# Adding exponential tiles on VectorE before the softmax sums, in chosen units of a fused attention + leaky-ReLU MLP kernel

## The chip, the cores and the metric

The kernel runs on one core of one Trainium2 chip. The metric is the device time of one execution in microseconds (us), the median of several runs. Within the core five engines work side by side, each from its own in-order queue of instructions: PE (TensorE, matrix products), DVE (VectorE), ACT (ScalarE), POOL (GpSimd) and SP (which issues DMA here). They meet only through semaphores: an instruction waits until what it needs has been written, or until what it overwrites has been read. Tile pools give each tile a buffer, and a pool with fewer buffers than tiles makes the next user wait for the last one.

## The reference

Eight batches of 12 heads, 448 positions, head width 64; then an MLP from 768 to 2048 and back on the 3584 rows that the attention gives.

```python
def rmsnorm(x, g):
    rms = np.sqrt(np.mean(x * x, axis=-1, keepdims=True) + 1e-06)
    return x / rms * g
q_n, k_n = (rmsnorm(q, g_q), rmsnorm(k, g_k))
scores = 1.0 / np.sqrt(64) * np.matmul(q_n, k_n.transpose(0, 1, 3, 2))
scores = scores - np.max(scores, axis=-1, keepdims=True)
attn = np.exp(scores)
attn = attn / (np.sum(attn, axis=-1, keepdims=True) + 1e-09)
attn_out = np.matmul(attn, v)                      # 8 x 12 x 448 x 64
x = attn_out.transpose(0, 2, 1, 3).reshape(3584, 768)
h = x @ w_in                                       # 768 x 2048
g = np.maximum(0.01 * h, h)
out = g @ w_out                                    # 2048 x 768
```

## The kernel before

The work is cut into 24 units `u` of four heads each (three units make a batch). A unit has seven key tiles; the exponentials of key tile `t` stand in `et[:, t]`, 128 partitions (keys) by 2 x 448 fp16. Units are pipelined: while unit `u` forms scores and exponentials in four steps `d` = 0 to 3 (key tile 0; 1 and 2; 3 and 4; 5 and 6), PE also sums and multiplies the exponentials of unit `u-1`, and in the gaps it runs items of the MLP of an earlier batch from a queue (`fill`). The program order on each engine is fixed by the order of these calls.

The parts that matter here: the softmax sums over keys are matrix products with ones. `zcol` serves units 4 to 22, `zsum_slot` the last (and the first few).

```python
def zcol(u):                       # sums of unit u: 7 tiles x 4 matmuls
    s = st[u]
    s["zc"] = aux([P, 512], FP32, "zc")
    for t in range(NS):            # NS = 7
        for y in range(2):
            for a in range(2):
                c = 32 * (2 * y + a)
                nc.tensor.matmul(s["zc"][c:c + 32, 0:HS], onesr, s["et"][:, t, a, HS * y:HS * y + HS],
                                 start=(t == 0), stop=(t == NS - 1))       # 224 columns each

def shift_max(u):                  # the row shift of unit u, from its first score tile
    ...
    nc.vector.tensor_reduce(s["spare"][:, 511:512], sT[:, :, 0:S], axis=AXL.XY, op=ALU.max)
    s["dg"] = small.tile([P, P], FP16, tag="dg", name="dg")
    nc.vector.tensor_tensor(s["dg"], ident16, s["spare"][:, 511:512].broadcast_to([P, P]), op=ALU.mult)

def shift_mm(u):                   # spreads it over the partitions
    ...
    for x in range(2):
        nc.tensor.matmul(pb[:, x], onesp, s["dg"][:, 64 * x:64 * x + 64], start=True, stop=True)
    nc.vector.tensor_reduce(s["spare"][:, 510:511], pb, axis=AXL.XY, op=ALU.max)
    ...
```

The norms and the scaling of the attention's output on GpSimd:

```python
def prep_rinv(u, tis=BOTH):        # 1/rms on ACT
    nc.scalar.activation(buf(u, "uu")[:, x], buf(u, "ssq")[:, x], AF.Ln, bias=eps_t, scale=1.0 / D)
    nc.scalar.activation(buf(u, "rinv")[:, x], buf(u, "uu")[:, x], AF.Exp, bias=0.0, scale=-0.5)

def prep_norm(u, ...):             # n = x * rinv on DVE, two inputs in SBUF
    nc.vector.tensor_tensor(buf(u, "n16")..., src[...], buf(u, "rinv")...broadcast_to(...), op=ALU.mult)

def xmul_pool(u, eng=nc.gpsimd):   # xt = x32 * rz, two inputs in SBUF
    ...
    eng.tensor_tensor(xts[b][:, g], s["x32"], s["rz"], op=ALU.mult)
```

The second half of the MLP as seven products; `later` puts an evacuation off to the next item, `flush` issues what was put off. The third product adds to the bank `ma` that the copy put off by the first one has to have read:

```python
def i0():
    flush()
    g["o"] = (out_tile(), out_tile())
    mm(bank("ma"), gblock(tt[0], 0), wblock(0, 0), True)
    later(lambda: nc.vector.tensor_copy(g["o"][1][:, L], g["ma"][:, 0:HC]))
def i1():
    flush()
    mm(bank("mb"), sa[:, 1], tw[:, 1], True)
    later(lambda: add(g["o"][1][:, L], g["o"][1][:, L], "mb"))
    ...
def i2():
    flush()
    mm(g["ma"], gblock(tt[0], 1), wblock(1, 0), False)      # accumulates into ma
    ...
```

The loop, cut to what is needed:

```python
for u in range(3, NU):             # NU = 24
    for d in range(4):
        qk(u, STEPS[d])            # scores, PE
        if d == 0:
            shift_max(u)           # DVE
            ...
            pv_slot(u - 1)         # attention times v, PE, 28 matmuls
            zcol(u - 1)            # PE
            shift_mm(u)            # PE, waits for dg
            pv_out(u - 1)          # x32, ACT, waits for the shift
        ex(u)                      # exponentials, ACT
        ...
        jobs = []                  # d == 1: prep_ssq(u+2);  d == 2: prep_rinv(u+2), prep_norm(u+2), its transposes
        ...
        fill(u, d, jobs)           # MLP items from the queue, one job after each
zsum_slot(NU - 1)
pv(NU - 1)
...
```

Of the kernel before, what the change touches and what calls it, by code (L numbers as in the profile page):

```python
# [8 lines left out]
FP32 = mybir.dt.float32  # L9
FP16 = mybir.dt.float16  # L10
AF = mybir.ActivationFunctionType
ALU = mybir.AluOpType
# [6 lines left out]
def kernel(  # L19
# [11 lines left out]
    nc = tc.nc  # L31

    B, H, S, D = q.shape
    QH = 4
    NS = 7
    P = 128
    NQ = H // QH
    NU = B * NQ
# [6 lines left out]
    cst = ctx.enter_context(tc.tile_pool(name="cst", bufs=1))  # L45
# [4 lines left out]
    zpool = ctx.enter_context(tc.tile_pool(name="zpool", bufs=1))  # L50
# [6 lines left out]
    def aux(shape, dtype, name):  # L57
        if held:
            return held[0].pop(0)
        return psum.tile(shape, dtype, tag="aux", bufs=4, name=name)  # L60
# [6 lines left out]
    def drop(bank):  # L67
        if held:
            held[0].append(bank)
# [3 lines left out]
    ones16 = cst.tile([P, D], FP16)  # L73
    nc.vector.memset(ones16, 1.0)
    onesr = cst.tile([P, 32], FP16)
# [6 lines left out]
    nc.vector.memset(eps_t, 1.0e-6)  # L82
    one32 = cst.tile([1, 1], FP32)
    nc.vector.memset(one32, 1.0)
    grow = cst.tile([1, 2, D], FP32)
    gdup = cst.tile([1, 2, D], FP32)
    gcol = cst.tile([P, 1], FP32)
    gate_t = cst.tile([P, 1], FP16)
    vts = [cst.tile([P, 2, NS, D], FP16, name=f"vt{i}") for i in range(NV)]
# [21 lines left out]
    st = {}  # L111
# [51 lines left out]
    def prep_norm(u, c=ALL, tis=BOTH):  # L163
        n = c[1] - c[0]
        for ti in tis:
            src = raw[u][ti]
            nc.vector.tensor_tensor(  # L167
                buf(u, "n16")[:, ti, c[0]:c[1]].rearrange("p s a d -> p a s d"), src[:, :, c[0]:c[1]],
                buf(u, "rinv")[:, ti, :, c[0]:c[1], None].broadcast_to([P, 2, n, D]), op=ALU.mult)
# [19 lines left out]
    def slot():  # L189
        return psum.tile([P, 2, 512], FP32, tag="sT", bufs=2, name="sT")  # L190
# [7 lines left out]
    def qk(u, steps):  # L198
        st[u]["sT"] = []
        for t in steps:  # L200
            sT = slot()
            score(u, t, (sT[:, 0], sT[:, 1]))
            st[u]["sT"].append((t, sT))
# [17 lines left out]
    def shift_max(u):  # L221
        s = st[u]
        sT = s["sT"][0][1]
        if isinstance(sT, list):
            pm2 = small.tile([P, 2], FP32, tag="pm2", name="pm2")
            for a in range(2):
                nc.vector.tensor_reduce(pm2[:, a:a + 1], sT[a][:, 0:S], axis=AXL.X, op=ALU.max)
            s["spare"] = sT[0]
            nc.vector.tensor_reduce(s["spare"][:, 511:512], pm2, axis=AXL.X, op=ALU.max)
        else:  # L230
            s["spare"] = sT[:, 0]
# [3 lines that stand above are left out]
# [25 lines left out]
    def zsum(u, t0=0, t1=NS):  # L260
        s = st[u]
        for t in range(t0, t1):
            for r in range(2):
                for a in range(2):
                    nc.tensor.matmul(s["zt"][r][64 * a:64 * a + 64, 0:S], ones16[64 * r:64 * r + 64],
                                     s["et"][64 * r:64 * r + 64, t, a], start=(t == 0), stop=(t == NS - 1))

    def zsum_slot(u):
        s = st[u]
        s["zslot"] = slot()  # L270
        s["zt"] = [s["zslot"][:, r] for r in range(2)]
        zsum(u)

    HS = S // 2

    def zcol(u):
        s = st[u]
        s["zc"] = aux([P, 512], FP32, "zc")
        for t in range(NS):
            for y in range(2):  # L280
                for a in range(2):
                    c = 32 * (2 * y + a)
                    nc.tensor.matmul(s["zc"][c:c + 32, 0:HS], onesr, s["et"][:, t, a, HS * y:HS * y + HS],  # L283
                                     start=(t == 0), stop=(t == NS - 1))

    def pv_slot(u):
        s = st[u]
        s["pslot"] = slot()
        s["pv"] = [s["pslot"][:, r] for r in range(2)]
        pv(u)  # L290

    def pv_out(u):
        s = st[u]
        s["x32"] = zpool.tile([P, 2, S], FP32, tag="x32", name="x32")
        nc.scalar.copy(s["x32"], s["pslot"][:, :, 0:S])  # L295

    def zcol_ln(u):
        s = st[u]
        s["zs"] = zpool.tile([P, HS], FP32, tag="zs", name="zs")
        nc.scalar.activation(s["zs"], s["zc"][:, 0:HS], AF.Ln)  # L300
        drop(s["zc"])

    def zcol_inv(u):
# [3 lines left out]
        for r in range(2):  # L307
            for y in range(2):
                src = s["zs"][64 * y + r:64 * y + 64:2, None, :]
                nc.sync.dma_start(s["rz"][:, r, HS * y:HS * y + HS], src.broadcast_to([32, 4, HS]))  # L310

    def xmul_sb(u):
        xmul_pool(u, nc.vector)
# [382 lines left out]
    def narrow(u):  # L696
        return 4 <= u < NU - 1
# [46 lines left out]
    with tc.manual_schedule():  # L744
# [182 lines left out]
        for u in range(3, NU):  # L927
            for d in range(4):
                if d > 0 or u > 3:
                    qk(u, STEPS[d])  # L930
                    if d == 0:
                        shift_max(u)
                        if u == 6:
                            xmul_sb(u - 2)
                        if narrow(u - 1):
                            pv_slot(u - 1)
                            zcol(u - 1)
                            shift_mm(u)
                            pv_out(u - 1)
                        else:  # L940
                            zsum_slot(u - 1)
                            pv(u - 1)
                            shift_mm(u)
                            zinv(u - 1)
                    ex(u)
                    if d == 0 and narrow(u - 1):
                        zcol_ln(u - 1)
                jobs = []

                def job(fn, *args):  # L950
                    jobs.append(lambda: fn(*args))

                if d == 0:
                    if u == 3:
                        prep_norm(4)
                        gate(4)
                    elif narrow(u - 1):
                        if u < NU - 1:
                            job(zcol_inv, u - 1)
                    else:  # L960
                        xmul(u - 1)
                    if u + 4 < NU:
                        job(load, u + 4)
                    if u + 3 < NU:
                        load_v(u + 3)
                    if u < 6:
                        prep_sqp(u + 3)
                if d == 1 and narrow(u - 1) and not 5 <= u < 8 and u < NU - 1:
                    xmul_pool(u - 1)
                if u == NU - 1:  # L970
                    if d == 1:
                        job(zcol_inv, u - 1)
                    if d == 2:
                        xmul_pool(u - 1)
                if fed(u, d) and u > 3:
                    push(u // NQ - 1)
                if (u, d) in ((3, 1), (4, 0)):
                    for ti in range(2):
                        prep_tr(u + 1, ti, VV)
                if d == 1 and 5 <= u < NU - 1:  # L980
                    job(prep_g, u + 1)
                if u + 2 < NU:
                    if d == 1:
                        for ti in range(2):
                            job(prep_ssq, u + 2, ALL, (ti,))
                    if d == 2:
                        job(prep_rinv, u + 2)
                        for ti in range(2):
                            job(prep_norm, u + 2, ALL, (ti,))
                        if u > 3:  # L990
                            job(prep_trd, u + 2)
                if d == 1 and 4 <= u < 8:
                    job(weight_sum, u - 4, 0)
                if d == 0 and 5 <= u < 9:
                    job(weight_sum, u - 5, 1)
                if d == 2 and 6 <= u < 8:
                    job(xmul_sb, u - 1)
                if u == NU - 2 and d == 0:
                    for n, tile_ in ((1, (raws, "rq", 3)), (2, (raws, "rk", 3)), (3, None), (4, (prep_p, "sq", 3))):
                        job(win_sum, n, 1, tile_)  # L1000
                    for n in (3, 1, 2, 4):
                        job(x_sum, LATE, n)
                if d == 3 and 6 <= u < NU - 3:
                    for ti in range(2):
                        job(prep_sq, u + 3, ALL, (ti,))
                fill(u, d, jobs)
# [4 lines left out]
        for i, ns in enumerate(((3, 1), (2, 4))):  # L1011
            c, fn = queue[i]
# [33 lines left out]
```

## Time and profile before

| | |
|---|---|
| time, median of 3 runs | 422.28 us (421.82 to 422.55) |
| span of the profiled execution | 420.3 us |
| granted TensorE clock, mean | 0.992 |
| POOL line 320, `xt<-x,rz` | 16 times, 2085 ns each |
| ACT line 214, the exponentials, 128x896 | 166 times, 1010 ns each |
| PE line 283, the sums `zc` | 504 records of 224 columns |

How to read it: the profile is one execution. A group's row names line, engine, operation and tiles, then the busy time, the mean length of one, and the idle time of the engine just before it with the instruction that ended the idle time. The timeline gives start and length in us. Engines run in order, so an idle time on one engine says what it waited for next, not that it had nothing further down its queue. Only what delays the engine that is never idle, or the chain of waits that ends last, changes the time.

### The profile page before, as it was taken

To read this page: it belongs to the slowest core of one execution; us is meant where nothing else is said; L and a number is where in the kernel's file an instruction comes from. 1 tells how busy PE (TensorE), PEld (TensorE's weight loads), DVE (VectorE), ACT (ScalarE), POOL (GpSimd) and SP (SyncE) were. 2 spreads that over 40 slices of the span, in tenths; PEclk is the share of its full clock that TensorE was granted. 3 is DMA by queue.
4 is the path that set the end of the run, shared out by engine and by line. 5 is a ranking of instruction groups with operands and counts; after the bars stand their busy time and mean duration, and the time that the engine had idled before them with its cause. 6 is when DMAs were issued, how large, how long until landed. Compare 5 with 4: busy or idle time off the path is not lost.

```text
span 420.3 us, 9568 instructions
## 1 busy us (share of the span) xinstructions
PE 404.4 (96%) x3959; PEld 222.9 (53%) x3959; DVE 269.2 (64%) x440; ACT 303.6 (72%) x474; POOL 83.0 (20%) x75
## 2 busy tenths in 40 slices
PE   7977999999999999999999999999999999999995
PEld 6544444555445544555445544455445557558853
DVE  5788665787658736466448745467338787527762
ACT  5999878868987689867986779967986657653600
POOL 1958422300020111210121111120101101010000
PEclk9699999999999999999999999999999999999999
DMA  8999999889664795678565796578562460032023
GB/s 257 218 239 237 235 250 147 200 156 215 169 153 68 224 212 120 168 163 180 152 130 107 194 203 150 151 141 170 180 111 44 121 155 11 7 78 75 2 53 100
DMA packets 71951, 62.42 MB, mean 149 GB/s; under 512 B 36324, under 2 KB 67044, under 8 KB 71908
## 3 DMA queue, kind: packets, MB, share of 16 engines
q1 hardware_dynamic: 61312, 49.62, 47.2%
q0 software_dynamic: 10272, 11.80, 18.1%
q8 instruction: 31, 0.51, 0.5%
q10 hardware_dynamic: 324, 0.39, 0.3%
q14 instruction: 12, 0.10, 0.1%
HBM read 45.61 MB, written 11.01 MB: 135 GB/s over the span
## 4 chain that ended last, share of the span: by engine, by line
PE 83%; ACT 8%; DVE 6%; issue 1%; DMA 1%; SPq 0%; DVEq 0%; ACTq 0%
PE hps L362 27%; PE sT L195 8%; PE sT L340 6%; PE ma L444 5%; PE md L444 5%; PE mc L444 5%; ACT et L214 5%; PE bank L444 5%; PE bank L564 4%; PE op L403 3%; PE zc L283 3%; PE mb L444 3%; DVE n L167 2%; PE sT L444 2%; PE bank L403 1%
## 5 line engine op out<-in xcount | busy, mean ns | idle before, releaser
L214 ACT ACTIVATE et<-sT,eb 128x896 f16<-128x896 f32 x166 | 159.4, 1010 | 18.6 <-PE sT L195 16.9
L362 PE MATMUL hps<-xt,win 128*128 128x448 f16 x600 | 120.8, 353 | 0.2 <-DVE xt L349 0.2
L362 PEld LDWEIGHTS <-win 128*128 128x128 f16 x612 | 56.8, 98 | 58.2 <-issue 9.6
L320 POOL TENSOR_TENSOR xt<-x,rz 128x896 f16<-128x896 f32 x16 | 33.4, 2085 | 148.0 <-DMA rz<-zs 139.5
L356 ACT ACTIVATE gt<-hps 128x448 f16<-128x448 f32 x100 | 54.0, 556 | 6.1 <-PE hps L362 5.4
L167 DVE TENSOR_TENSOR n<-rq,rinv 128x896 f16<-128x896 f32 (+2 forms) x25 | 27.2, 1090 | 47.0 <-ACT rinv L161 44.2
L195 PE MATMUL sT<-qkT 64*64 64x448 f16 x664 | 53.2, 369 | 3.0 <-ACT et L214 1.9
L155 DVE TENSOR_REDUCE ssq<-sq 128x14 f32<-128x896 f32 (+2 forms) x49 | 50.3, 1058 | 1.6 <-ACT sq L144 1.6
L444 PEld LDWEIGHTS <-sa 128*128 128x128 f16 x352 | 32.8, 98 | 26.3 <-issue 6.1
L295 ACT COPY x<-sT 128x896 f32<-128x896 f32 x19 | 17.2, 906 | 36.4 <-DVE sT L245 36.4
L124 POOL DMA_DIRECT2D vt<-in_v_dram x24 | 18.2, 757 | 114.9 <-PE sT L340 107.4
L444 PEld LDWEIGHTS <-gt 128*128 128x128 f16 x264 | 25.2, 98 | 18.7 <-issue 2.1
L195 PEld LDWEIGHTS <-qkT 64*64 64x64 f16 x672 | 15.2, 105 | 36.8 <-issue 33.5
L340 PE MATMUL sT<-et,vt 64*64 64x448 f16 x532 | 28.5, 350 | 0.3
L403 PE MATMUL op<-wout,gt 128*128 128x384 f16 x160 | 28.4, 327 | 0.0
L232 DVE TENSOR_REDUCE sT<-sT 128x1 f32<-128x896 f32 x22 | 24.1, 1093 | 4.3 <-PE sT L195 4.3
L340 PEld LDWEIGHTS <-vt 64*64 64x64 f16 x672 | 20.7, 107 | 11.3 <-issue 1.7
L167 DVE TENSOR_TENSOR n<-rk,rinv 128x896 f16<-128x896 f32 (+2 forms) x26 | 26.1, 1009 | 0.0
L403 PEld LDWEIGHTS <-gt 128*128 128x128 f16 x192 | 17.6, 98 | 14.3 <-issue 3.0
L444 PE MATMUL ma<-wout,gt 128*128 128x384 f16 x128 | 23.5, 326 | 0.0
L425 DVE TENSOR_TENSOR sa<-gt 128x512 f16<-128x512 f16 (+1 forms) x15 | 8.2, 544 | 18.5 <-ACT gt L356 13.9
L144 ACT ACTIVATE sq<-rq 128x896 f32<-128x896 f32 (+2 forms) x18 | 16.3, 913 | 1.3 <-DMA rq<-in_q_dram 1.3
(135 smaller groups left out, 516.6 us busy)
## 6 DMA issues: line engine op xcount, KB each, us to landing
rq<-in_q_dram SPq DMA_DIRECT2D x24, 448.0 KB, 3.9
rk<-in_k_dram SPq DMA_DIRECT2D x24, 448.0 KB, 5.6
out_dram<-ost SPq DMA_DIRECT2D x52, 192.0 KB, 3.3
rz<-zs SPq DMA_DIRECT2D x76, 112.0 KB, 2.3
vt<-in_v_dram POOLq DMA_DIRECT2D x24, 224.0 KB, 5.1
win<-in_moe_w_in_dram POOLq DMA_DIRECT2D x8, 384.0 KB, 16.8
wout<-in_moe_w_out_dram POOLq DMA_DIRECT2D x2, 1536.0 KB, 29.7
out_dram<-ost SPq DMA_DIRECT2D x4, 96.0 KB, 2.1
```

The lines of the kernel that those rows point to most:

```text
L124: nc.gpsimd.dma_start(vts[u % NV].rearrange("p a t d -> p a (t d)"), rows(v, u))
L155: nc.vector.tensor_reduce(buf(u, "ssq")[:, ti, :, c[0]:c[1]], buf(u, f"sq{ti}")[:, :, c[0]:c[1]], axis=AXL.X, op=ALU.add)
L167: nc.vector.tensor_tensor(buf(u, "n16")[:, ti, c[0]:c[1]].rearrange("p s a d -> p a s d"), src[:, :, c[0]:c[1]], buf(u, "rinv")[:, ti, :, ...
L195: nc.tensor.matmul(banks[a][64 * r:64 * r + 64, 0:S].rearrange("p (t x) -> p t x", t=NS), kT(u, r, a, t), qT(u, r, a), start=True, stop=True)
L214: nc.scalar.activation(s["et"][:, t], sT[:, :, 0:S], AF.Exp, bias=s["eb"], scale=1.0)
L232: nc.vector.tensor_reduce(s["spare"][:, 511:512], sT[:, :, 0:S], axis=AXL.XY, op=ALU.max)
L320: eng.tensor_tensor(xts[b][:, g], s["x32"], s["rz"], op=ALU.mult)
L340: nc.tensor.matmul(s["pv"][r][64 * a:64 * a + 64, 0:S], vts[u % NV][64 * r:64 * r + 64, a, t], s["et"][64 * r:64 * r + 64, t, a], start=(t ...
L356: nc.scalar.activation(dst, src, AF.Prelu, bias=0.0, scale=1.0, alpha=0.01)
L362: nc.tensor.matmul(hps[:, 0:S], win16[:, kt // 2, kt % 2, ts(ft, P)], xt[:, kt // 2, kt % 2], start=(kt == 0), stop=(kt == KT - 1))
L403: nc.tensor.matmul(op2[:, 0:HC], gt[:, ft, ds(col(t), P)], wout16[:, ft, ds(HC * half, HC)], start=(ft == 0), stop=(ft == FT - 1))
L444: nc.tensor.matmul(bank[:, 0:HC], a[:, f], b[:, f], start=(first and f == 0), stop=(f == HF - 1), skip_group_check=not first)
```

## The change

In twelve units VectorE adds some of the seven exponential tiles into one fp16 tile `ea` first, so that the product with ones has fewer tiles to sum: in nine units five tiles are added (four additions), in three units three tiles (two additions). The product then takes the remaining `et` tiles and `ea` last. It is meant to use time in which VectorE stood idle in step 2 for the norms' reciprocals, and to take matmuls off PE. The sums are those of the same exponentials, with the partial sums rounded to fp16.

```diff
-    grow = cst.tile([1, 2, D], FP32)
-    gdup = cst.tile([1, 2, D], FP32)
+    g_t = zpool.tile([P, 2, S], FP32, tag="x32", name="g_t")          # room for ea
+    grow = g_t[0:1, 0, 0:2 * D].rearrange("p (a d) -> p a d", a=2)
+    gdup = g_t[0:1, 1, 0:2 * D].rearrange("p (a d) -> p a d", a=2)
@@ zsum_slot
-        zsum(u)
+        ets = z_tiles(u)
+        for i, e in enumerate(ets):
+            ... the same matmuls with e in place of et[:, t] ...
@@
+    ADDED = {8: 3, 14: 3, 20: 3, NU - 1: 5}
+    ADDED.update({u: 5 for u in (4, 7, 10, 11, 13, 16, 17, 19)})
+
+    def add_e(u):
+        s = st[u]
+        s["ea"] = zpool.tile([P, 2, S], FP16, tag="ea", name="ea")
+        for t in range(1, ADDED[u]):
+            nc.vector.tensor_tensor(s["ea"], s["et"][:, 0] if t == 1 else s["ea"], s["et"][:, t], op=ALU.add)
+
+    def z_tiles(u):
+        s = st[u]
+        ets = [s["et"][:, t] for t in range(NS)]
+        return ets[ADDED[u]:] + [s["ea"]] if "ea" in s else ets
@@ zcol
-        for t in range(NS):
+        ets = z_tiles(u)
+        for i, e in enumerate(ets):
             for y in range(2):
                 for a in range(2):
                     c = 32 * (2 * y + a)
-                    nc.tensor.matmul(s["zc"][c:c + 32, 0:HS], onesr, s["et"][:, t, a, HS * y:HS * y + HS],
-                                     start=(t == 0), stop=(t == NS - 1))
+                    nc.tensor.matmul(s["zc"][c:c + 32, 0:HS], onesr, e[:, a, HS * y:HS * y + HS],
+                                     start=(i == 0), stop=(i == len(ets) - 1))
@@ the loop, after ex(u)
+                if d == 2 and u in ADDED and u < NU - 1:
+                    add_e(u)
@@ the loop, among the jobs
+                if u == NU - 1 and d == 3:
+                    job(add_e, u)
```

So in units 4 to 20 the additions stand in VectorE's queue at the start of step 2, before the norms of that step; in the last unit they stand in step 3. In the order of instructions of the changed kernel the two additions of units 14 and 20 stand directly after the second `ssq` and before the copy of `ma`, those of unit 8 after that copy and after two of the MLP's block sums, before the addition of `mb`.

More of the change, by code (lines that the diff above doesn't have):

```diff
@@ L271, in zsum_slot @@
         s["zt"] = [s["zslot"][:, r] for r in range(2)]
-        zsum(u)
-    HS = S // 2
+        ets = z_tiles(u)
+        for i, e in enumerate(ets):
+            for r in range(2):
+                for a in range(2):
+                    nc.tensor.matmul(s["zt"][r][64 * a:64 * a + 64, 0:S], ones16[64 * r:64 * r + 64],
+                                     e[64 * r:64 * r + 64, a], start=(i == 0), stop=(i == len(ets) - 1))
+    HS = S // 2
+    ADDED = {8: 3, 14: 3, 20: 3, NU - 1: 5}
[9 more added lines that the diff above has]
+        return ets[ADDED[u]:] + [s["ea"]] if "ea" in s else ets
     def zcol(u):
```

## The prediction

> **What bounds the kernel now.** I read the page's busy shares first, then the chain of waits, then the timeline around one hand-over between units, then the collisions of DVE and POOL.
>
> ```profile
> PE 404.4 (96%) x3959; PEld 222.9 (53%) x3959; DVE 269.2 (64%) x440; ACT 303.6 (72%) x474; POOL 83.0 (20%) x75
> ...
> PE 83%; ACT 8%; DVE 6%; issue 1%; DMA 1%; SPq 0%; DVEq 0%; ACTq 0%
> ```
>
> PE is the bound: 96% busy, 83% of the chain. A matmul taken off PE shortens the time only if PE does not meet another wait instead; and anything that stops PE is added, as it has no slack to catch up with. Each hand-over from unit u to u+1 looks like this one (13 to 14):
>
> ```profile
> 210.50 0.29 DVE L234 TENSOR_TENSOR dg<-ident,sT 128x128 f16<-128x128 f16 x1
> 210.50 0.85 PE L283 MATMUL zc<-et,onesr 128*32 128x224 f16 x28
> ...
> 211.29 0.23 PE L244 MATMUL sT<-dg,onesp 128*128 128x64 f16 x2
> ```
>
> The shift matmul (line 244) needs `dg`, ready at 210.50 + 0.29 = 210.79, and comes when the 28 sum matmuls are through, at 211.29. So the sums hide DVE here with 0.50 us to spare. The smallest distance anywhere is 0.05 us (into unit 8, where PE really waits), so the usable slack is what exceeds 0.05.
>
> The waits list puts the change's target in one line, the reciprocals that DVE waits for:
>
> ```profile
> DVE n L167 <- ACT rinv L161: 44.2, 15, 6.6
> ```
>
> But POOL's product works in the same stretch, and it and DVE stop one another:
>
> ```profile
> 156.66 2.08 POOL L320 TENSOR_TENSOR xt<-x,rz 128x896 f16<-128x896 f32 x1 [7.91 <-DMA rz<-zs]
> 158.21 1.48 DVE L167 TENSOR_TENSOR n<-rq,rinv 128x896 f16<-128x896 f32 x1 [6.63 <-ACT rinv L161]
> ```
>
> The norm takes 1.08 us elsewhere; here 1.48, ending 1.08 after 158.61, that is 0.13 before POOL's record ends (158.74). Unit 14 shows the same, and what the additions will stand in front of:
>
> ```profile
> 219.15 2.10 POOL L320 TENSOR_TENSOR xt<-x,rz 128x896 f16<-128x896 f32 x1 [7.50 <-DMA rz<-zs]
> 219.22 1.08 DVE L155 TENSOR_REDUCE ssq<-sq 128x14 f32<-128x896 f32 x1
> 219.55 1.46 PE L444 MATMUL mb<-tw,sa 128*128 128x384 f16 x8
> 220.22 0.55 DVE L460 COPY ost<-ma 128x384 f32<-128x384 f32 x1
> ...
> 220.68 0.85 DVE L431 TENSOR_TENSOR sa<-gt 128x512 f16<-128x512 f16 x1
> ...
> 220.85 1.46 PE L444 MATMUL ma<-wout,gt 128*128 128x384 f16 x8
> ```
>
> The block sum of line 431 (0.42 us when free) took 0.85; the reduce and the PSUM copy, with one SBUF input or none, ran on. PE's second `ma` follows the copy by 0.08 us: it accumulates into the bank that the copy reads.
>
> **What the Trainium skill says.** "SBUF — State Buffer", section "Who interferes with whom": a VectorE instruction with two SBUF inputs and a GpSimd instruction that reads SBUF exclude one another for the whole instruction, whichever came first. The two rows above agree: 1.48 for 1.08 us, 0.85 for 0.42. "VectorE: DVE Perf Modes", section "What auto-detection actually checks": a two-source addition of 16-bit tiles reaches two elements per cycle, not four. The block sums agree: 0.42 us for 512 and 0.68 for 1024 columns is 0.51 ns a column. "TensorE: Matmul & The Clock Gate", section "Wait — 56ns, not 53.3ns?": matmuls start no closer than about 25 ns. The 28 sum matmuls take 0.785 us in the chain, 28 ns each, so removing one saves 28 ns, although four of them run side by side.
>
> **The change part by part.**
> 1. Removed. Five tiles added leave 3 of 7 tiles: 16 matmuls less, 16 x 28 = 0.45 us. Three added leave 5: 8 less, 0.22 us. The last unit's 28 (1.45 us on the chain) lose 16, 0.8 us. Were all of it gained: 8 x 0.45 + 3 x 0.22 + 0.8 = 5.1 us.
> 2. Added. 8 x 4 + 3 x 2 + 4 = 42 additions of 128x896 fp16. By 0.42 us plus 384 further columns at 0.51 ns: 0.62 us each, 0.65 from start to start as each needs the last. 26 us of DVE in all, which DVE's 64% can hold; the question is where.
> 3. The hand-overs after the 5-tile units, each from the timeline. Slack (`dg` ready to shift matmul) is 0.50, 0.50, 0.50, 0.50 after units 4, 13, 16, 19: after the 0.05 that is needed, 0.45 stays, the whole saving. Their additions end before, or by up to about 0.75 us after, the reciprocals are there, and DVE has 0.2 to 0.8 us of idle time later in these units before the reduce. Gain 4 x 0.45 = 1.8 us. After unit 7 the slack is 0.05: PE waits for `dg` already, gain 0.
> 4. Unit 10: tiles 1 and 2 are exponentiated by 154.06, tile 3 by 156.40, tile 4 by 157.29. The third addition goes at 156.43 to 157.05 and holds POOL off; POOL then holds the ports to about 158.9, and the fourth runs to 159.5. The norm moves to 159.4 (it ran from 158.61), the norms end 0.8 us later, the reduce 0.3. Gain about 0.14.
> 5. Units 11 and 17. Here the collision has no room:
>
> ```profile
> 170.88 2.07 POOL L320 TENSOR_TENSOR xt<-x,rz 128x896 f16<-128x896 f32 x1 [7.51 <-DMA rz<-zs]
> ...
> 172.84 1.09 DVE L167 TENSOR_TENSOR n<-rq,rinv 128x896 f16<-128x896 f32 x1 [5.26 <-ACT rinv L161]
> ...
> 177.86 0.29 DVE L234 TENSOR_TENSOR dg<-ident,sT 128x128 f16<-128x128 f16 x1
> ...
> 178.27 0.23 PE L244 MATMUL sT<-dg,onesp 128*128 128x64 f16 x2
> ```
>
>    ACT's row for tiles 3 and 4 starts at 170.01 (two in 1.90 us), so tile 3 is there at 171.02, and POOL has started at 170.88. The third addition waits to 172.82 and ends at 173.44, the fourth at 174.1, so the norm starts 1.17 us late. From there to `dg` DVE has 0.2 us of idle time. `dg` is ready at 178.15 + 1.17 - 0.2 = 179.1, the shift matmul at 179.15 in place of 178.27: 0.9 us lost, twice 1.8.
> 6. Unit 8: two additions (1.19 us with overlaps) go between the block sums and the addition of `mb`, where DVE is behind and has only 0.22 us of idle time until the reduce. `dg` moves from 131.85 to 132.8, the shift matmul from 132.28 to 132.86: 0.6 us lost.
> 7. Units 14 and 20: the two additions come before the copy of `ma` and collide with POOL. From the fence above: POOL lets go at 221.12, the additions end at 221.74 and 222.39, the copy (PSUM, may overlap 0.08) at 222.86. PE's second `ma` starts at about 222.9 in place of 220.85: 2.06 us lost. DVE's later work moves by about as much, so the slack of 0.43 stays and 0.22 comes back. 1.84 lost, twice 3.7.
> 8. The last unit: POOL's last product (370.64, 2.08 us) lets go at 372.6, so four additions end at 375.2; PE starts its sums at 374.50, has 0.4 us of work on tiles 5 and 6, waits 0.3. Gain 0.5 of 0.8.
>
> Sum: 1.8 + 0.14 + 0.5 = 2.4 gained; 1.8 + 0.6 + 3.7 = 6.1 lost. Net 3.6 us slower, 425.9. I take 425.5, since the smaller collisions could come out shorter than I set them.
>
> **The rivals.**
> (a) All the saving is gained, or nearly: 417.2 to 418.5. For it: 44.2 us of idle time against 26 us of additions, and the additions stand before the wait. Against it: three of the hand-overs after 5-tile units have slack under 0.1 us beyond the need (units 7, 11, 17), and in units 8, 14, 20 the waits list shows no reciprocal wait at all: DVE's idle 5 us there ends before the additions, at the first block sum.
> (b) The hand-over absorbs the saving, but nothing blocks: POOL and DVE do not exclude one another for fp16 additions. Then units 14 and 20 lose only two additions in front of the copy, 1.19 - 0.05, less 0.22, about 0.9 each; units 11 and 17 gain 0.07 each; unit 10 0.45; the last 0.75. Sum: gained 3.1, lost 0.6 + 1.8 = 2.4; 421.6, no difference. The 1.48 and 0.85 rows speak against it.
> (c) The end of a DVE delay spreads: the transposes of the norms come later, and the next unit's scores wait. The prefetch is two units ahead and DVE waits 9.3 us for transposed tiles in 7 places without stopping PE, so I give this little: 427 to 428.
>
> **Range and chances.** 8 in 10 between 420.5 and 428.5: the low end is rival (b) and a bit, the high end (c). Over 2% would be 8.4 us either way; the whole saving is 5.1, so faster by that is all but excluded (0.01); slower by it needs twice my losses (0.03). Within 2%: 0.96.
>
> **What would show it.** Step 1: `zc` records fall by 8 x 16 + 3 x 8 = 152, and by none more. Step 2: additions of 0.62 us when free, and over 1 us where POOL's row overlaps. Step 3: shift matmuls 0.05 us after `dg` in most changed units. Step 5: DVE's norm in units 11 and 17 starts over 1 us after the reciprocals. Step 7: PE idle about 2 us before the second `ma` of units 14 and 20, released by the copy of line 460's counterpart. I am wrong if PE stands at most 0.3 us before those `ma`, or if POOL's product in the changed units runs elsewhere than beside the third addition, for instance because its transfer lands later.

## The result, and the profile after

| | before | after |
|---|---|---|
| time, median of 4 runs each | 422.31 us (421.82 to 422.55) | 427.19 us (426.76 to 427.55) |
| ratio to before, 95% interval | | 1.0117 [1.0099, 1.0134] |
| span of the profiled execution | 420.3 us | 425.4 us |
| granted TensorE clock, mean | 0.992 | 0.992 |

The change makes the kernel 1.2% slower. The page of the changed kernel, with the engines' busy times and then the chain of waits by engine:

```profile
PE 401.5 (94%) x3791; PEld 220.2 (52%) x3791; DVE 303.7 (71%) x482; ACT 303.6 (71%) x474; POOL 83.0 (20%) x75
...
PE 65%; DVE 17%; ACT 11%; issue 3%; DMA 2%; SPq 1%; DVEq 0%; ACTq 0%
```

PE lost 168 instructions (152 of the `zc` sums and 16 of the last unit's) and 2.9 us of busy time, and DVE got 34.5 us more for 42 additions. That is more than 42 x 0.62 = 26 us: the rest is time in which an addition, or a norm, is on record as running but stands. The chain shows the price: DVE's share of it went from 6% to 17%.

The waits list still has a row for the norms, and it has shrunk from 44.2 us to 4.0. A second row shows what DVE waits for instead (columns: engine and line, releaser, us in total, times, longest):

```profile
DVE ea L288 <- ACT et L215: 17.9, 17, 2.5
...
PE sT L245 <- DVE dg L235: 4.2, 6, 1.3
DVE n L168 <- ACT rinv L162: 4.0, 10, 1.0
```

So the idle time was filled, as the change meant it to be. But PE now waits for `dg` in six places, up to 1.3 us. Where the time went is read at the hand-overs. Below, a step is the time from the shift matmul of one unit to that of the next, less the same step in the kernel before; the step into unit u+1 shows what was done to unit u. All are worked out from the timelines' rows of lines 244 and 245.

| step into unit | additions in the unit before it | predicted, us | measured, us |
|---|---|---|---|
| 5 | 4 (unit 4) | -0.45 | -0.38 |
| 8 | 4 (unit 7) | 0 | 0.01 |
| 9 | 2 (unit 8) | +0.6 | +0.56 |
| 11 | 4 (unit 10) | -0.14 | 0.00 |
| 12 | 4 (unit 11) | +0.9 | +0.90 |
| 14 | 4 (unit 13) | -0.45 | +0.02 |
| 15 | 2 (unit 14) | +1.84 | +1.85 |
| 17 | 4 (unit 16) | -0.45 | -0.37 |
| 18 | 4 (unit 17) | +0.9 | +0.96 |
| 20 | 4 (unit 19) | -0.45 | -0.38 |
| 21 | 2 (unit 20) | +1.84 | +1.87 |
| shift of unit 23 to the end | 4 (unit 23) | -0.5 | +0.47 |

The last row counts to the end of the trace, 420.26 us before and 425.41 after. The rows add up to 5.51 us; the steps not listed lie between -0.06 and +0.11. The span grew by only 5.15, because `dg` of unit 4, which no addition precedes, began 0.35 us earlier in this execution (57.43 for 57.78). That moment lay between 56.65 and 57.86 in the profiles of this study, so it says nothing of the change; it is left out of the first row.

A hand-over that gained, from unit 4 to 5, in the timeline of the changed kernel (start and length in us):

```profile
72.24 0.38 PE L303 MATMUL zc<-et,onesr 128*32 128x224 f16 x8
72.24 0.29 DVE L235 TENSOR_TENSOR dg<-ident,sT 128x128 f16<-128x128 f16 x1
72.44 0.27 PE L303 MATMUL zc<-ea,onesr 128*32 128x224 f16 x4
...
72.64 0.23 PE L245 MATMUL sT<-dg,onesp 128*128 128x64 f16 x2
```

Twelve sum matmuls (8 on `et`, 4 on `ea`) take 0.40 us of the chain in place of 28 in 0.79, and `dg`, ready at 72.53, still comes in time. Then the places that lose. Unit 11, where the third addition meets POOL:

```profile
170.65 2.07 POOL L340 TENSOR_TENSOR xt<-x,rz 128x896 f16<-128x896 f32 x1 [7.46 <-DMA rz<-zs]
170.85 3.08 DVE L288 TENSOR_TENSOR ea<-ea,et 128x896 f16<-128x896 f16 x2 [1.28 <-ACT et L215]
...
172.39 0.23 ACT L162 ACTIVATE rinv<-uu 128x28 f32<-128x28 f32 x1
...
173.85 1.08 DVE L168 TENSOR_TENSOR n<-rq,rinv 128x896 f16<-128x896 f32 x1
...
178.65 0.29 DVE L235 TENSOR_TENSOR dg<-ident,sT 128x128 f16<-128x128 f16 x1
178.99 0.22 PE L245 MATMUL sT<-dg,onesp 128*128 128x64 f16 x2 [1.23 <-DVE dg L235]
```

Two additions take 3.08 us, since the first of them stands until POOL is through. The reciprocals are there at 172.62, and the norm begins 1.23 us later. PE comes to the shift matmul and waits 1.23 us for `dg`. Unit 14:

```profile
219.87 2.08 POOL L340 TENSOR_TENSOR xt<-x,rz 128x896 f16<-128x896 f32 x1 [7.53 <-DMA rz<-zs]
...
220.93 1.51 DVE L288 TENSOR_TENSOR ea<-et 128x896 f16<-128x896 f16 x1
...
222.47 0.62 DVE L288 TENSOR_TENSOR ea<-ea,et 128x896 f16<-128x896 f16 x1
223.01 0.55 DVE L480 COPY ost<-ma 128x384 f32<-128x384 f32 x1
...
223.62 1.46 PE L464 MATMUL ma<-wout,gt 128*128 128x384 f16 x8 [1.89 <-DVE ost L480]
```

The second `ma` waits 1.89 us for a copy that itself needs nothing that the additions make: it only stands behind them in DVE's queue. By the rows, about 0.9 of these 1.89 us is the first addition standing (1.51 for 0.62 us), and the rest the two additions themselves. The experiments tell the two apart.

### The profile page after: what moved, and what is told of

The parts are those of the page before. It is cut to its first block, busy times and chain, and to the rows that moved or that the text cites. A ratio compares the mean times of both kernels' runs of the same rounds, so it can differ in the third digit from the quotient of the medians.

```text
span 425.4 us, 9300 instructions
## 1 busy us (share of the span) xinstructions
PE 401.5 (94%) x3791; PEld 220.2 (52%) x3791; DVE 303.7 (71%) x482; ACT 303.6 (71%) x474; POOL 83.0 (20%) x75
## 4 chain that ended last, share of the span: by engine, by line
PE 65%; DVE 17%; ACT 11%; issue 3%; DMA 2%; SPq 1%; DVEq 0%; ACTq 0%
PE hps L382 21%; ACT et L215 7%; PE sT L196 6%; PE md L464 5%; PE mc L464 5%; DVE n L168 5%; PE bank L584 4%; PE bank L464 4%; PE ma L464 4%; PE sT L360 4%; DVE ea L288 3%; PE op L423 3%; DVE sT L233 2%; DMA rk<-in_k_dram 2%; PE zc L303 2%
## 5 line engine op out<-in xcount | busy, mean ns | idle before, releaser
L288 DVE TENSOR_TENSOR ea<-ea,et 128x896 f16<-128x896 f16 x30 | 26.5, 884 | 15.4 <-ACT et L215 13.9
```

The lines of the kernel that those rows point to most:

```text
L288: nc.vector.tensor_tensor(s["ea"], s["et"][:, 0] if t == 1 else s["ea"], s["et"][:, t], op=ALU.add)
```

## The experiments

The theory: 1. a matmul taken away is worth something, but less than 28 ns; 2. most of the loss comes from POOL's product holding up DVE's instructions with two SBUF inputs (the reverse, POOL held up by DVE, comes to 0.11 us at most in any run: 2.19 for 2.08 us); 3. the rest comes from additions that stand in DVE's queue before work that PE needs. The rivals: (a) as a time, 417.2 to 418.5 us, is excluded by the result; what can be left of it is that the saving is close to the full 5.1 us and something else is lost; (b) there is no such exclusion, and only the order in DVE's queue counts; (c) a delay on DVE spreads into the units that follow.

| run | time, us | before on the same chip, us | ratio [95%] |
|---|---|---|---|
| no_14_20 | 422.34 | 421.81 | 1.0009 [0.9997, 1.0021] |
| no_11_17 | 425.70 | 421.81 | 1.0097 [1.0068, 1.0126] |
| memset_before | 421.34 | 421.81 | 0.9996 [0.9983, 1.0008] |
| memset_after | 420.20 | 421.81 | 0.9962 [0.9949, 0.9975] |
| sums_only | 418.15 | 421.97 | 0.9908 [0.9894, 0.9922] |
| copy_first | 425.29 | 421.97 | 1.0074 [1.0061, 1.0088] |
| moved_3 | 422.40 | 421.97 | 1.0010 [1.0000, 1.0020] |
| best | 420.18 | 421.97 | 0.9948 [0.9936, 0.9961] |
| best_again | 419.66 | 422.28 | 0.9944 [0.9927, 0.9961] |
| after_again | 426.84 | 422.28 | 1.0120 [1.0101, 1.0139] |

All edits are against the changed kernel, but for memset_before.

**Units 14 and 20 without additions (no_14_20).**

```diff
-    ADDED = {8: 3, 14: 3, 20: 3, NU - 1: 5}
+    ADDED = {8: 3, NU - 1: 5}
```

> The changed kernel without the additions of units 14 and 20. Theory A (the additions stand in front of the copy of ma, and PE's second ma waits for that copy): the stalls of 1.85 and 1.87 us at these two hand-overs go, 427.2 - 3.7 = 423.5 us. Theory B (the loss is spread over all additions, because VectorE is fuller): 4 of 42 additions carry a tenth of the loss, about 426.7 us.

The steps into 15 and 21 went to -0.01 and 0.00; those into 9, 12 and 18 stayed (0.56, 0.90, 0.96). The step into 14 gained its 0.38 and the end lost 0.04 only, and neither was touched (what moves these two is told below, under steps 3 and 8). Without four of the 42 additions nearly all of the net loss is gone: the ratio falls from 1.0117 to 1.0009.

**Units 11 and 17 without additions (no_11_17).**

```diff
-    ADDED.update({u: 5 for u in (4, 7, 10, 11, 13, 16, 17, 19)})
+    ADDED.update({u: 5 for u in (4, 7, 10, 13, 16, 19)})
```

> The changed kernel without the additions of units 11 and 17. Theory A (GpSimd's product holds off the third addition there, the norms come late and the hand-over waits for dg): the steps of 0.90 and 0.96 us into units 12 and 18 go back to about 0, 427.2 - 1.9 = 425.3 us. Theory B (loss spread over all additions): 8 of 42 additions, about 426.2 us.

The steps into 12 and 18 fell to -0.01 and 0.00, so the two 0.9 us are these units' own. Yet the whole fell by less than 1.86 us: +0.44 appeared into 13, +0.45 into 20 (-0.38 in the changed kernel), and the step into 21 grew from 1.87 to 2.44. Into 13 is the telling one, because unit 12 has no additions in any kernel. Its timeline in no_11_17:

```profile
186.57 2.08 POOL L340 TENSOR_TENSOR xt<-x,rz 128x896 f16<-128x896 f32 x1 [8.84 <-DMA rz<-zs]
...
187.53 2.07 DVE L168 TENSOR_TENSOR n<-rq,rinv 128x896 f16<-128x896 f32 x1 [0.31 <-ACT rinv L162]
...
190.12 1.46 PE L464 MATMUL md<-tw,gt 128*128 128x384 f16 x8 [0.29 <-DVE ost L471]
```

POOL's product began 9.19 us after its hand-over, against 7.56 in the kernel before, because its `rz` transfer landed later. So it fell on the norm, which took 2.07 in place of 1.08 us. A collision is thus not a property of a unit alone: it is a matter of where POOL's product falls, and that differs from kernel to kernel.

**POOL reads nothing (memset_before, memset_after).** POOL's product is replaced, in the kernel before and in the changed one, by writing ones at the same place in the program. The scaling of the attention's output in these units is left out.

```diff
-        eng.tensor_tensor(xts[b][:, g], s["x32"], s["rz"], op=ALU.mult)
+        if eng is nc.gpsimd:
+            nc.gpsimd.memset(xts[b][:, g], 1.0)
+        else:
+            eng.tensor_tensor(xts[b][:, g], s["x32"], s["rz"], op=ALU.mult)
```

> The kernel before, with GpSimd's products of units 7 to 22 replaced by a fill of the same tile with 1.0 on GpSimd, which reads nothing: the scaling is left out. It is the control of the next run. The one place in the kernel before where GpSimd's product delays a hand-over is the norm of unit 15 (1.70 us in place of 1.08): up to 0.6 us less, 421.7 to 422.3 us.

> The changed kernel with the same fill in place of GpSimd's products (the scaling is left out). Theory A (exclusion of VectorE's two-input additions and GpSimd's reading product): every addition takes 0.62 us, units 11 and 17 cost nothing, units 14 and 20 cost about 0.9 us each in place of 1.85, units 10 and 13 and the last unit gain 0.4 to 0.7: about 421 us, 0.2 to 1.2 us under the control. Theory C (the additions are slow or late for another reason, such as waiting for the exponentials): no change against the changed kernel, about 427 us.

The fill does not wait for `rz`. It took 0.86 us and began 0.2 to 0.7 us after most hand-overs, where the product took 2.08 and began 7.5 us or more after them. So both runs take POOL out of step 2 altogether, and no addition lies beside a fill. Six block sums of memset_after do, each with two inputs in SBUF, and they keep their usual 0.42 us (512 columns) or 0.68 us (1024), as here:

```profile
176.87 0.86 POOL L341 MEMSET xt<- 128x896 f16 x1
...
177.16 0.68 DVE L454 TENSOR_TENSOR sa<-gt 128x1024 f16<-128x1024 f16 x1
```

The control shows no clear difference: in the kernel before, POOL's product in step 2 cost nothing measurable that reached PE. In the changed kernel it is worth 1.0117 - 0.9962 = 1.55%, 6.5 us. The additions by duration in ns, smallest, median, largest, first in the changed kernel:

```profile
L288 DVE TENSOR_TENSOR ea<-ea,et x30: 624/626/2489, 66.0 to 380.1; 128x896 f16<-128x896 f16 x30
L288 DVE TENSOR_TENSOR ea<-et x12: 611/625/1983, 65.2 to 376.6; 128x896 f16<-128x896 f16 x12
```

and in memset_after:

```profile
L288 DVE TENSOR_TENSOR ea<-ea,et x30: 624/624/626, 65.3 to 372.8; 128x896 f16<-128x896 f16 x30
L288 DVE TENSOR_TENSOR ea<-et x12: 610/616/626, 64.6 to 370.7; 128x896 f16<-128x896 f16 x12
```

No addition is stretched any more. That the stretched ones stood, and were not merely slowed, is seen in the changed kernel itself: nine additions overlap POOL's product there. They began 0.07 to 1.73 us after it, and all nine end 0.48 to 0.49 us after its record ends, as if each had started 0.13 us before that end and then run its 0.62. The Trainium skill ("SBUF — State Buffer", section "Who interferes with whom") calls it an exclusive lock on a shared pair of ports, and the trace agrees for fp16 additions as well: rival (b) falls. So the engines do not meet only through semaphores: DVE and POOL meet here as well. What is left of unit 14 is the order alone, in the timeline of memset_after:

```profile
218.04 0.61 DVE L288 TENSOR_TENSOR ea<-et 128x896 f16<-128x896 f16 x1
...
218.69 0.62 DVE L288 TENSOR_TENSOR ea<-ea,et 128x896 f16<-128x896 f16 x1
219.23 0.55 DVE L483 COPY ost<-ma 128x384 f32<-128x384 f32 x1
...
219.83 1.46 PE L467 MATMUL ma<-wout,gt 128*128 128x384 f16 x8 [1.00 <-DVE ost L483]
```

The wait fell from 1.89 to 1.00 us, and the steps into 15 and 21 from 1.85 and 1.87 to 0.96 and 0.97. Half of it was the lock, half the place in the queue.

**The matmuls gone, nothing added (sums_only).** The additions are left out and with them part of the softmax sum: four of the seven tiles (or two) are never summed.

```diff
-        return ets[ADDED[u]:] + [s["ea"]] if "ea" in s else ets
+        return ets[ADDED[u] - 1:] if u in ADDED else ets
-                if d == 2 and u in ADDED and u < NU - 1:
-                    add_e(u)
-                if u == NU - 1 and d == 3:
-                    job(add_e, u)
```

> The changed kernel without any addition: the sums simply leave out the tiles that would have been added (part of the softmax sum is left out). It shows how much PE time the removed matmuls are worth when nothing is paid for it. Counted at 28 ns a matmul and all gained: 5.1 us, ratio 0.988. Counted at the 23 ns that the hand-overs show (0.37 us for 16), and only as far as dg is not awaited (0 after unit 7, 0.06 after 11 and 17): 5 x 0.37 + 2 x 0.06 + 3 x 0.19 + 0.75 = 3.3 us, ratio 0.992.

This is all that fewer matmuls can bring: 0.92%, 3.8 us (3.5 by the steps of its profile), not the 5.1 of step 1. Rival (a) falls. By steps: -0.37 to -0.39 after units 4, 10, 13, 16 and 19 (16 matmuls: 23 to 24 ns each), -0.19 to -0.21 after units 8, 14 and 20 (8 matmuls), -0.07 after 11 and 17 (they have 0.12 of slack, of which 0.05 is needed), nothing after 7, and -0.77 at the end. Were no `dg` awaited after 7, 11 and 17, these sizes would come to 8 x 0.38 + 3 x 0.19 + 0.77 = 4.4 us.

The three ratios split the result: fewer matmuls -0.92%; the additions in DVE's queue +0.54% (0.9962 - 0.9908), that is 2.3 us; the lock +1.55%, 6.5 us. Each ratio carries about 0.13 to 0.17% of its own; the steps of the profiles give -3.5, +2.6 and +6.4 us. The split holds for these kernels as they fell; it isn't a law of three independent terms, as no_11_17 shows.

**The copy before the additions (copy_first).** In units 14 and 20 the two additions go behind the copy of `ma` and two block sums.

```diff
-                if d == 2 and u in ADDED and u < NU - 1:
+                if d == 2 and u in ADDED and u not in (14, 20) and u < NU - 1:
                     add_e(u)
+                # on the job of prep_rinv:
+                        if u in (14, 20):
+                            jobs[-1] = also(jobs[-1], lambda: later(add_e, u))
```

> The changed kernel with the two additions of units 14 and 20 put behind the copy of ma (and the two block sums that follow), as they stand in unit 8. Theory A (PE's second ma waits for the copy): the two hand-overs cost about 0.6 us each, as after unit 8, in place of 1.85: 2.5 us less than the changed kernel, ratio to before about 1.006. Theory D (the two additions cost the same wherever they stand in step 2): no change, ratio 1.012.

In unit 14 the `ma` wait is gone, in the timeline of copy_first:

```profile
220.50 0.55 DVE L480 COPY ost<-ma 128x384 f32<-128x384 f32 x1
220.96 1.15 DVE L451 TENSOR_TENSOR sa<-gt 128x512 f16<-128x512 f16 x1
222.03 0.41 DVE L454 TENSOR_TENSOR sa<-gt,sa 128x512 f16<-128x512 f16 x1
222.37 0.61 DVE L288 TENSOR_TENSOR ea<-et 128x896 f16<-128x896 f16 x1
...
228.69 0.29 DVE L235 TENSOR_TENSOR dg<-ident,sT 128x128 f16<-128x128 f16 x1
```

DVE has no idle time between these additions and `dg`, so `dg` comes late instead. PE waits 0.99 us for it, and the step into 15 is still +0.85, that into 21 +0.58. Moving the additions behind the first wait halved the loss and moved the rest to the next wait. Another 0.67 us appeared into 22; the next run shows what that is.

**The two additions a step earlier (moved_3).** In units 8, 14 and 20 they stand in step 1, where the waits list of before shows DVE idle.

```diff
-                if d == 2 and u in ADDED and u < NU - 1:
+                if d == 2 and ADDED.get(u) == 5 and u < NU - 1:
                     add_e(u)
-                        for ti in range(2):
-                            job(prep_ssq, u + 2, ALL, (ti,))
+                        job(prep_ssq, u + 2, ALL, (0,))
+                        if ADDED.get(u) == 3:
+                            jobs[-1] = also(jobs[-1], lambda: add_e(u))
+                        job(prep_ssq, u + 2, ALL, (1,))
```

> The changed kernel with the two additions of units 8, 14 and 20 moved to step 1, behind the first ssq, where VectorE idles 5 us for the MLP's last activation (tile 2 is there about 1 us before that idle time ends). Theory A: these hand-overs gain 0.19 us each in place of losing 0.56, 1.85 and 1.87: 4.8 us less than the changed kernel, ratio to before about 1.000. Theory B (loss spread over all additions): no change, ratio 1.012.

The timeline of moved_3 in unit 14:

```profile
216.61 0.62 DVE L288 TENSOR_TENSOR ea<-et 128x896 f16<-128x896 f16 x1 [2.55 <-ACT et L215]
...
217.51 0.62 DVE L288 TENSOR_TENSOR ea<-ea,et 128x896 f16<-128x896 f16 x1 [0.27 <-ACT et L215]
...
218.51 0.43 DVE L445 TENSOR_TENSOR sa<-gt 128x512 f16<-128x512 f16 x1 [0.38 <-ACT gt L376]
```

Both additions lie in what was idle time, with 0.38 us to spare before the block sum. The steps into 9, 15 and 21 turn from +0.56, +1.85 and +1.87 into -0.21, -0.21 and -0.18: the full worth of eight matmuls. The ratio is 1.0010 all the same, since units 11 and 17 still lose 0.90 and 0.96, and 0.80 appeared into 22, after a unit without additions. It looks like a delay that spread, rival (c), but the timeline of moved_3 in unit 21 shows another collision:

```profile
333.21 2.08 POOL L340 TENSOR_TENSOR xt<-x,rz 128x896 f16<-128x896 f32 x1 [16.00 <-DMA rz<-zs]
```

```profile
333.81 2.43 DVE L168 TENSOR_TENSOR n<-rq,rinv 128x896 f16<-128x896 f32 x1 [0.31 <-ACT rinv L162]
```

POOL began 9.56 us after the hand-over, in the kernel before 7.52, where it was through before the norm and the norm took 1.09. copy_first has the same (9.42 us after, a norm of 2.31 us).

**What is left when each place is chosen (best, best_again, after_again).** best keeps five tiles only in 4, 16 and 19, three tiles in 10 and 13, and the early place for 8, 14 and 20. It leaves 7, 11 and 17 alone, and in the last unit puts two additions in step 2, ahead of POOL's product. best_again and after_again are best and the changed kernel again on another chip, side by side.

```diff
+    ADDED = {8: 3, 14: 3, 20: 3, 10: 3, 13: 3, NU - 1: 3}
+    ADDED.update({u: 5 for u in (4, 16, 19)})
+    EARLY = (8, 14, 20)                       # step 1, as in moved_3
...
+                if u == NU - 1 and d == 2:    # in place of d == 3
+                    job(add_e, u, (1,))
+                    job(add_e, u, (2,))
```

> Additions only where dg and the copy leave room: five tiles in units 4, 16 and 19; three in 10 and 13 (both additions before GpSimd's product starts); three in 8, 14 and 20 in step 1; three in the last unit, in step 2; none in 7, 11, 17. Theory A: gains of 0.37 x 3 + 0.19 x 5 + 0.37 = 2.4 us on the kernel before, ratio 0.994. Theory B (every addition costs): 3 x 4 + 6 x 2 = 24 additions, slower than before by over 1 us, ratio 1.003 or more.

> The same kernel as best, once more, to see whether the loss of 1.0 us into unit 12 (no additions in unit 11; GpSimd's product started 1.3 us later after the hand-over than in the kernel before, 9.18 for 7.86 us, and held off the norm) belongs to the kernel or to the execution. If to the execution (the issue of the small transfers of rz takes 0.5 to 2.0 us): the product starts at 7.8 to 7.9 us after that hand-over and the step into unit 12 is about 0; other units may be hit. If to the kernel: 9.2 and 1.0 again. Time in both cases 0.993 to 0.996 of before.

> The changed kernel once more beside it. Steps into 9, 12, 15, 18, 21 of 0.56, 0.90, 1.85, 0.96, 1.87 us again, as the order of the instructions fixes them; the step into unit 14 (0.02, where 0.37 was to be gained) between -0.4 and 0.1, depending on when GpSimd's product of that unit starts. Ratio about 1.012.

It beats both kernels: 0.9948 and 0.9944, some 2.3 us faster than before and 7 us faster than the change. 24 additions do it. In after_again the steps into 9, 12, 15, 18 and 21 came back within 0.01 us, and the step into 14 was -0.38. One place of best still loses, in both executions: +1.01 and +0.62 into unit 12, though unit 11 has no additions. (In best the step into 11 lost 0.12 in the same way, with POOL at 9.33 us after its hand-over; in best_again it gained 0.19.) The timeline of best, unit 11:

```profile
171.20 2.07 POOL L342 TENSOR_TENSOR xt<-x,rz 128x896 f16<-128x896 f32 x1 [8.93 <-DMA rz<-zs]
...
171.83 2.39 DVE L168 TENSOR_TENSOR n<-rq,rinv 128x896 f16<-128x896 f32 x1 [4.69 <-ACT rinv L162]
```

As in unit 12 of no_11_17, POOL's product comes late (9.18 us after the hand-over for 7.86; 8.79 in best_again, between the two cases expected) and the norm stands behind it. SP's queue shows a part of the reason, first the kernel before and then best:

```profile
166.51 2.49 SPq L310 DMA_DIRECT2D rz<-zs  x4
```

```profile
165.50 3.85 SPq L332 DMA_DIRECT2D rz<-zs  x4
```

The same four issues took 3.85 us in best (3.46 in best_again) and 2.49 before. One of the four makes the difference: 1.97 and 1.58 us, where the others took 0.5 to 0.6. Why it takes longer was not found; it stays open. It is not the only way to be late: in unit 12 of no_11_17 the issues took 2.49 us as before, and the transfer landed later.

## Why the prediction was right, and where its steps were not

The time, 427.19 us, lies in the range, 1.7 us above the number; the direction and the main mechanism are right: PE bounds the kernel, the saving is capped at the hand-overs, and the losses are DVE work held up by POOL or by its place in the queue. Step by step:

1. The saving was mis-sized: a sum matmul was set at 28 ns, by dividing a group's time by 28. In the records of the kernel before, the four matmuls of a tile start within about 10 ns of one another, and the next four about 96 ns later. So 16 matmuls less are four times 96 ns, the 0.37 to 0.38 us that were measured; the seven fours make 0.67 of the 0.79 us, and the other 0.12 us is a fixed part that stays. The prediction also quoted the Trainium skill ("TensorE: Matmul & The Clock Gate", section "Wait — 56ns, not 53.3ns?"), by which matmuls start no closer than about 25 ns. The starts here, 3 to 4 ns apart within a four, differ from it, and the measurement decides; that 96 / 4 = 24 ns comes near is no support for it. All matmuls together are worth 3.8 us, not 5.1.
2. Right: 0.61 to 0.63 us when free, up to 2.49 when blocked.
3. Right for 4, 16, 19 and 7 but for the size above (-0.38 for -0.45). Wrong for 13: +0.02. POOL's product began 8.78 us after its hand-over there, 7.91 before, with one `rz` issue of 1.47 us for 0.6. The same additions in other runs show that this start decides: at 8.18 (no_14_20) and 8.28 (after_again) the step gained 0.38, as predicted less the same size; at 8.66 (moved_3) it gained 0.10, and at 8.86 (copy_first) it lost 0.11. The step assumed that POOL stays where it was.
4. Wrong, by 0.14 us: POOL's product came before the third addition, not after it (7.95 us after the hand-over for 8.27), so DVE lost all that PE gained:

```profile
156.16 2.07 POOL L340 TENSOR_TENSOR xt<-x,rz 128x896 f16<-128x896 f32 x1 [7.60 <-DMA rz<-zs]
156.23 3.22 DVE L288 TENSOR_TENSOR ea<-ea,et 128x896 f16<-128x896 f16 x2 [1.71 <-ACT et L215]
```

5. Right: +0.90 and +0.96 for 0.9 each, and gone when the additions of 11 and 17 are.
6. Right: +0.56 for 0.6.
7. Right: +1.85 and +1.87 for 1.84, with the lock and the place in the queue carrying half each, as memset_after shows.
8. Wrong, and the largest miss: a gain of 0.5 was predicted, 0.47 was lost (0.94 in after_again). The last unit in the timeline of the changed kernel:

```profile
375.97 2.09 POOL L340 TENSOR_TENSOR xt<-x,rz 128x896 f16<-128x896 f32 x1 [21.42 <-DMA rz<-zs]
...
378.64 2.08 DVE L288 TENSOR_TENSOR ea<-ea,et 128x896 f16<-128x896 f16 x3
379.18 0.57 PE L277 MATMUL sT<-et,ones 64*64 64x448 f16 x8
...
380.78 0.38 PE L277 MATMUL sT<-ea,ones 64*64 64x448 f16 x4 [1.03 <-DVE ea L288]
```

   PE waits 1.03 us for `ea`, where 0.3 was set. The saving was sized rightly (0.77 us in sums_only for 0.8); the wait was not. POOL's product began 12.68 us after the shift matmul of unit 23, 12.03 before, because one of its four `rz` issues took 1.25 us. Six runs have these four additions in step 3 beside that product, and the end follows its start almost one to one: -0.22, +0.04, +0.47, +0.52, +0.92 and +0.94 us for starts at 12.01 (no_11_17), 12.26, 12.68, 12.72, 13.14 and 13.18. So with POOL where the prediction had it, 0.22 us would have been gained. The missing 0.28 goes for the most part to the additions after the first, which start 0.73 us apart here (378.64, 379.37, 380.11) where 0.65 was set. In best, with two additions in the step before, the sums wait for nothing and the end gains 0.38 us (61.27 us from that shift for 61.65).

Against the 3.6 us of the prediction's own sum the steps gave 5.51. Of these 1.9 us, the size of the saving in units 4, 16 and 19 made 0.2, unit 13 0.47, unit 10 0.14 and the last unit 0.97, 1.8 in all. That after_again gave nearly the same sum, 5.48, is chance: unit 13 gained there, and the end lost more. Taking 0.4 us off "since the smaller collisions could come out shorter" went the wrong way. Where POOL's product would start was the weak term: the prediction named this among its signs of being wrong, but gave it no cost. Of the rivals, (a) and (b) are excluded; (c) was not seen: in the change no more than +0.11 into 22, and where more appeared behind an edit, in copy_first and moved_3, it was POOL's product on a norm.

## What to carry to other kernels

Idle time on an engine is worth something only if what is put there ends before the next thing that the bounding engine needs from it, so look at the row behind the gap and not at its sum: the same two additions cost 1.85 us in one place and gained 0.21 one step earlier. Work with two SBUF inputs on VectorE is to be kept clear of a GpSimd product like this one, whose start is set by a transfer and wanders: for the same unit by up to 2 us here (7.5 to 9.6 in unit 21). So leave a margin of that size, or place the work ahead of it. To value a removed instruction, take one that is missing from a group and not the group's time divided by its number.

## What was unexpected

- POOL's product starts when four `rz` transfers have landed: 7.5 to 9.6 us after the hand-over of a unit in the middle, for the same instructions. This moved losses of 0.4 to 1.0 us from unit to unit, even into units that no edit touched (unit 12 in no_11_17, unit 21 in copy_first and moved_3).
- A blocked addition is on record from when it begins to stand: its length grows (2.49 us for 0.62), and no idle time is shown before the next row. DVE's busy share rises by waiting: the 42 additions are on record for 37.1 us in the changed kernel and for 26.2 in memset_after, so 11 us of DVE's 303.7 are additions standing.
- In the kernel before, the same lock cost nothing measurable (0.9996 [0.9983, 1.0008] with POOL out of the way): the norm of unit 15 took 1.70 us beside POOL for 1.09, and the step into 16 shortened by only 0.06 without it. The slack at the hand-overs took the rest.
